# Two attention blocks on one core: V loaded through GpSimd's queue, loads in cycles of eight units, and one unit of eight transposed by the remainder's DMA

## The chip, the core and the metric

The kernel runs on one core of one Trainium2 chip. A core has TensorE (PE; its weight loads are listed as PEld), VectorE (DVE), ScalarE (ACT), GpSimd (POOL) and SyncE (SP), which run their own instruction streams and wait for each other on semaphores, and 16 DMA engines that move data between HBM and SBUF and within SBUF. The metric is the device time of one execution in microseconds. Before the change the median of three runs is 1215.2 us (1215.15 to 1217.5).

## What is computed

Two attention blocks A and B of the same shape, one after the other, with inputs of their own. The result is the concatenation of both along the last axis.

```
B, Sq, D = 16, 144, 448;  H, Sk, Dh = 16, 512, 256        # bf16
q      = (x @ wq).reshape(B, Sq, H, Dh).transpose(0, 2, 1, 3)
scores = einsum("bhqd,bhkd->bhqk", q, k_cache) * Dh ** -0.5
p      = softmax(scores, axis=-1)
o      = einsum("bhqk,bhkd->bhqd", p, v_cache)
out    = o.transpose(0, 2, 1, 3).reshape(B, Sq, H * Dh) @ wo
```

K and V are caches: 67 MB each for each block, read once.

## The kernel before

A *unit* is one pair of batch and head, 512 in all (256 for each block). Its 144 query rows are split in a main part of 112 rows (QA) and a *remainder* of 32 rows (QB). Four units' remainders fill 128 partitions, so the remainder is worked in groups G of four units, and two groups make a *cycle* SG of eight units (64 cycles).

What a unit goes through, with the lines of the kernel before:

- `t_q` (line 340): TensorE multiplies x by wq, eight matmuls into `qp_ps`; VectorE (353) or ScalarE (357) writes `qt_sb`.
- `t_sa` (476): the main part's scores, two matmuls into one of two `sa_ps` banks. `t_max` (488) on VectorE, `t_exp` (499) on ScalarE into `pa_sb`, `t_recip` (509) on VectorE, `t_norm` (517) on GpSimd, which multiplies P by the reciprocal of the row sum.
- `t_ta` (530): "TA", four transposes of P on TensorE into the `sa_ps` banks; `t_evac_pta` (540) copies them on VectorE into `pt_sb`.
- `t_pv` (563): P times V, eight matmuls into `ot_ps`; ScalarE (578, 580) writes them to `ring`.
- `t_op_piece` (601): the output projection, matmuls of `ring` with `wo_sb`, in pieces spread over the units; `t_evac_op` (619, 622) and `t_store` (630) write 36 blocks of rows.

For a cycle's remainder: `t_sb` (380) makes the scores of eight units in two `sb_ps` banks; `t_max_b` (393), `t_exp_b` (403), `t_recip_b` (413) and `t_norm_b` (421) make P in `pb_sb`. Its transpose goes one of two ways. In the cycles of the set `TB_SG`, `t_tb` (443, "TB") does it on TensorE and `t_evac_tb` (453) on VectorE copies it to `pbt_sb`. In the others `t_ptb_dma` (431) does it with a transposing DMA from SP, `pb_sb` to `pbt_sb`. In both ways `t_copy_ptb` (463) on GpSimd spreads it from `pbt_sb` into `pt_sb`, group by group.

Loads, all issued on SP's queue: `t_load_k` (307), a transposing DMA of 2 MB for a cycle; `t_load_v` (318), 1 MB for four units; `t_load_x` (297 and 298), two transposing DMAs for two batches (32 units); `t_load_wq` (276, 278) and `t_load_wo` (286).

The order is recorded by a loop over *slots* i (line 745 on). In slot i each engine's list gets the work of several units: the query projection of a unit about 8 further than the scores, the scores of unit i + lag, the norm of the unit whose scores were recorded one slot earlier, TA of unit i + 2 (`LT`), P V of unit i, and some pieces of the output projection. `LAGS` gives the lag by cycle: it begins at 7, drops to 5 and grows to 14. `sb_slot[SG]` is 8 SG - lag, the slot of the remainder's scores; `sa_slot[u]` that of a unit's scores. A small class (`_Sched`) derives the semaphore waits from what each instruction reads and writes, so a transfer into a buffer waits for the last reader of it. Each engine works through its list in order; SP too, so a load that waits holds up every load behind it.

When loads are recorded is planned in slots by `plan_x`, `plan_k`, `plan_v` and `plan_pb`. After the first eight cycles (`RAMP`) the plan runs in steps of two cycles (line 694): x, P, K, P, K and then four V in this order. There are two K buffers (`NK`), five V buffers (`NV`), fourteen for P (`NPA`), and one for `pbt_sb` (`NPBT`).

Of the kernel before, what the change touches and what calls it, by code (L numbers as in the profile page):

```python
# [122 lines left out]
def bass_concat_heads__mha_block_cached__gqa_block_cached__near_ridge_kernel(  # L123
# [24 lines left out]
    NU = Bn * H  # L148
# [14 lines left out]
    LAGS = (7, 5, 6, 7, 8, 9, 10, 11, 12, 13, 14)  # L163
    RAMP = 8
    TB_SG = set(range(RAMP)) | set(range(NSG // 2 - 4, NSG // 2 + 6))
    NK, NV, NXG = 2, 5, 2
    WO_AT = ((12, 18, 26, 33), (277, 277, 293, 293))
# [4 lines left out]
    NQT, NPA, NPB, NPT, NST, NSTB, NOST = 12, 14, 2, 8, 4, 2, 3  # L172
# [10 lines left out]
    with contextlib.ExitStack() as es:  # L183
# [14 lines left out]
        pb_sb = sb("pb_sb", [128, NPB, 2, SK], BF16)  # L198
        pt_sb = sb("pt_sb", [128, NPT, 4, SQ], BF16)
        pbt_sb = sb("pbt_sb", [128, NPBT, 2, 4, 128], BF16)  # L200
# [15 lines left out]
        for i in range(NV):  # L216
            sem_names.append("v%d" % i)
        for i in range(NXG):
            sem_names.append("xt%d" % i)
# [19 lines left out]
        def t_ident():  # L239
            ones = pa_sb[:, 0, 0:128]  # L240

            def e1(g):
                return g.memset(ones, 1.0)
            S.add(POOL, e1, writes=[(("pa", 0), "ones")], name="ones")

            def e2(g):
                return g.affine_select(ident[:], ones, pattern=[[1, 128]], compare_op=ALU.is_equal,
                                       fill=0.0, base=0, channel_multiplier=-1)
            S.add(POOL, e2, reads=[(("pa", 0), "ones")], writes=[("ident", 0)], name="ident")

# [61 lines left out]
        def t_load_v(G):  # L312
            pr, b, h0 = unit(4 * G)
            sl = G % NV
            src = vs[pr][b, h0:h0 + 4].rearrange("u (p c) d -> p u (c d)", p=128)

            def e(q):
                return q.dma_start(v_sb[:, sl, :, :], src).then_inc(sems["v%d" % sl], 16)
            S.add(SP, e, writes=[(("v", sl), G)], dma_sem="v%d" % sl, name="v%d" % G)
# [106 lines left out]
        def t_ptb_dma(SG):  # L426
# [3 lines left out]
            def e(q):  # L430
# [3 lines left out]
            S.add(SP, e, reads=[(("pb", psl, g), (2 * SG + g, 1)) for g in range(2)],  # L434
                  writes=[(("pbt", tsl, g), SG) for g in range(2)], dma_sem="pb%d" % tsl, name="pb%d" % SG)
# [56 lines left out]

        def t_exp(U):
            bank = U % 2
            sl = U % NST
            psl = U % NPA

            def e(a):
                return a.activation(pa_sb[0:QA, psl, :], sa_ps[bank][0:QA, :], AF.Exp,  # L499
                                    bias=stat[0:QA, NEG + sl:NEG + sl + 1], scale=1.0,  # L500
                                    accum_out=stat[0:QA, RSUM + sl:RSUM + sl + 1])
            S.add(ACT, e, reads=[(("sap", bank), ("s", U)), (("neg", sl), U)],
                  writes=[(("pa", psl), (U, 0)), (("rsum", sl), U)], banks=["sa%d" % bank], name="ex%d" % U)
# [8 lines left out]
        def t_norm(U):  # L512
            sl = U % NST
            psl = U % NPA

            def e(g):
                return g.tensor_tensor(pa_sb[0:QA, psl, :], pa_sb[0:QA, psl, :],  # L517
                                       stat[0:QA, RINV + sl:RINV + sl + 1].to_broadcast([QA, SK]), op=ALU.mult)
            S.add(POOL, e, reads=[(("pa", psl), (U, 0)), (("rinv", sl), U)], writes=[(("pa", psl), (U, 1))],
                  name="nm%d" % U)  # L520

        def t_ta(U):
            psl = U % NPA
# [114 lines left out]
        t_warm_zero()  # L638
        ta_bank = {}
        lag = [LAGS[min(n, len(LAGS) - 1)] for n in range(NSG)]  # L640
# [24 lines left out]
        def plan_k(at, SG):  # L665
            plan(at, sa_slot[8 * (SG - NK) + 7] + 1 if SG >= NK else s_min, sb_slot[SG], t_load_k, SG)
# [5 lines left out]
        def plan_pb(at, SG):  # L672
            if SG not in TB_SG:
                plan(at, sb_slot[SG] + 5, 8 * SG - 1, t_ptb_dma, SG)

        plan_x(s_min, 0)
        for hg in range(HG):
            plan(s_min + (0 if hg < 2 else 1), s_min, q_slot[4 * hg], t_load_wq, 0, hg)
            if hg == 1:
                plan_k(s_min, 0)  # L680
        plan_v(s_min + 2, 0)
        for n in range(1, RAMP + 2):
            at = max(sb_slot[n] - 6, sa_slot[8 * (n - NK) + 7] + 1) if n >= NK else s_min + 2
            if n == 3:
                plan_x(at, 1)
            if n == 6:
                plan_x(at, 2)
            plan_k(at, n)
            plan_v(at + 1, 2 * n - 1)
            plan_v(at + 1, 2 * n)  # L690
# [3 lines left out]
        for n in range(RAMP, NSG, 2):  # L694
            t = 8 * n
            XG = (t + 32) // (XB * H)
            if (t + 32) % (XB * H) == 0 and XG < NXGT:
                plan_x(t - 4, XG)
            plan_pb(t - 4, n)
            if n + 2 < NSG:  # L700
                plan_k(t - 3, n + 2)
            plan_pb(t + 2, n + 1)
            if n + 2 < NSG:
                plan_k(t + 2, n + 3)
            for j, at in enumerate((5, 5, 5, 8)):
                if 2 * n + 3 + j < NG:
                    plan_v(t + at, 2 * n + 3 + j)
        for hg in range(HG):
            lo = q_slot[NU - H + 4 * hg + 3] + 1
            plan((4.9, 4.9, 8, 11)[hg] + NU - 32, lo, q_slot[NU + 4 * hg], t_load_wq, 1, hg)  # L710
# [35 lines left out]
        while True:  # L746
# [16 lines left out]
            while stores and stores[0][1] <= i and (i % 16 in (9, 10, 11) or i >= NT - 4):  # L763
# [23 lines left out]
            if i % 8 == 1 and 0 <= i < NT:  # L787
                t_copy_ptb((i + 3) // 4)
            for u in sa_at.get(i - 1, ()):
# [3 lines left out]
            if 0 <= u < NT:  # L793
# [104 lines left out]
```

## Time and profile before

| | |
|---|---|
| median of three runs | 1215.2 us |
| the profiled execution | 1209.51 us |
| its span on the core | 1207.8 us |
| mean granted TensorE clock | 0.994 |
| DMA | 306.18 MB, 254 GB/s on the mean |

The rows of the costliest groups that the change touches:

| line, engine | operation | count | busy us | mean ns |
|---|---|---|---|---|
| 517 POOL | multiply P, main part | 512 | 531.4 | 1039 |
| 421 POOL | multiply P, remainder | 128 | 133.0 | 1039 |
| 463 POOL | copy `pbt_sb` to `pt_sb` | 128 | 78.0 | 610 |
| 530 PE | TA matmuls | 2048 | 185.9 | 212 |
| 443 PE | TB matmuls | 144 | 12.4 | 219 |
| 540 DVE | copy of TA | 512 | 191.0 | 373 |
| 453 DVE | copy of TB | 36 | 14.1 | 416 |
| 307 SP | K load, transposing DMA | 64 | | |
| 318 SP | V load | 128 | | |
| 431 SP | P of the remainder, transposing DMA | 46 | | |

The page gives for every engine the time in which it executes something, then the span in 40 slices, then the groups. TensorE's matmuls are pipelined, so the durations of a group overlap and add up to more than the time that they take on the chain. The chain of waits is followed back from the last instruction; it gives for each piece its start, its length and the engine and line. DMA issues are listed with the engine that issues them (SPq is SP's queue): the time of an issue is that of the queue's instruction, not that of the transfer; the time to landing is counted from the issue.

### The profile page before, as it was taken

The numbers are of one execution on the slowest core, as the hardware profiler recorded it, in microseconds if no ns is written. First come the engines' busy times: TensorE is split into PE (matmuls) and PEld (weight loads), VectorE is DVE, ScalarE is ACT, GpSimd is POOL, SyncE is SP. The second block draws the span as 40 slices with busy tenths as digits, with TensorE's granted clock in tenths as the row PEclk, the third lists the DMA queues.
The fourth block names the chain that finished last, engine by engine and source line by source line (L and its number), as shares of the span: only waits on it lengthen the run. The fifth ranks groups of instructions, "written<-read, shape, count | busy, mean of one in ns | idle before, by whom it ended". The sixth has DMA issues, their size and how long they took to land.

```text
span 1207.8 us, 33200 instructions
## 1 busy us (share of the span) xinstructions
PE 1167.9 (97%) x13612; PEld 875.3 (72%) x13612; DVE 743.6 (62%) x2088; ACT 747.8 (62%) x2213; POOL 727.0 (60%) x774
## 2 busy tenths in 40 slices
PE   6898999999999999999899999999999999999989
PEld 4676777777777777777577777777777777777766
DVE  3676666666666656666466665665666566566661
ACT  2565666666666666666466666666666666566662
POOL 1676576666666566666465665666666665666661
PEclk9999999999999999999899999999999999999999
DMA  9999999999999999999999899999999999999981
GB/s 243 284 262 294 283 277 188 253 264 269 268 283 206 264 253 293 259 263 245 288 249 255 249 265 277 261 279 251 268 236 248 253 292 274 231 251 252 249 207 56
DMA packets 679577, 306.18 MB, mean 254 GB/s; under 512 B 597504, under 2 KB 610304, under 8 KB 679424
## 3 DMA queue, kind: packets, MB, share of 16 engines
q1 hardware_dynamic: 679424, 304.05, 104.1%
q8 instruction: 107, 1.75, 0.6%
q14 instruction: 46, 0.38, 0.1%
HBM read 148.90 MB, written 4.13 MB: 127 GB/s over the span
## 4 chain that ended last, share of the span: by engine, by line
PE 81%; DMA 11%; POOL 3%; DVE 3%; SPq 1%; issue 1%; ACT 0%; DVEq 0%
PE ot_ps L563 18%; PE qp_ps L340 17%; PE sa_ps L476 17%; PE op_ps L601 16%; PE sa_ps L530 7%; DMA kt_sb<-in_B_k_cache_dram 6%; PE sb_ps L380 5%; DMA kt_sb<-in_A_k_cache_dram 5%; POOL pa_sb L517 2%; DVE stat L488 1%; SPq L307 1%; POOL pb_sb L421 1%; PE qp_ps L601 1%; PE sb_ps L443 0%; DVE qt_sb L353 0%
## 5 line engine op out<-in xcount | busy, mean ns | idle before, releaser
L517 POOL TENSOR_TENSOR pa_sb<-pa_sb,stat 112x512 bf16<-112x512 bf16 x512 | 531.4, 1039 | 453.0 <-DVE stat L509 427.4
L499 ACT ACTIVATE pa_sb<-sa_ps,stat 112x512 bf16<-112x512 f32 x512 | 352.1, 688 | 400.5 <-DVE stat L488 398.2
L488 DVE TENSOR_REDUCE stat<-sa_ps 112x1 f32<-112x512 f32 x512 | 353.8, 691 | 329.6 <-PE sa_ps L476 324.8
L340 PEld LDWEIGHTS qp_ps<-xt_sb,wq_sb 128*128 128x128 bf16 x4048 | 283.4, 98 | 81.6 <-DMA wq_sb<-in_A_wq_dram 3.6
L340 PE MATMUL qp_ps<-xt_sb,wq_sb 128*128 128x144 bf16 x4048 | 336.7, 226 | 5.0 <-DMA wq_sb<-in_A_wq_dram 4.7
L563 PE MATMUL ot_ps<-pt_sb,v_sb 128*128 128x144 bf16 x4096 | 341.5, 226 | 0.0
L476 PE MATMUL sa_ps<-kt_sb,qt_sb 128*112 128x512 bf16 x1024 | 312.6, 387 | 6.7 <-DVE pt_sb L540 5.2
L601 PE MATMUL op_ps<-wo_sb,ring 128*128 128x448 bf16 x1120 | 275.3, 353 | 0.0
L563 PEld LDWEIGHTS ot_ps<-pt_sb,v_sb 128*128 128x128 bf16 x4096 | 268.9, 98 | 0.4
L530 PEld LDWEIGHTS sa_ps<-ident,pa_sb 112*128 112x128 bf16 x2048 | 143.8, 97 | 119.0 <-ACT pa_sb L499 38.0
L540 DVE COPY pt_sb<-sa_ps 128x448 bf16<-128x448 bf16 x512 | 191.0, 373 | 19.8 <-PE sa_ps L530 19.8
L578 ACT ACTIVATE ring<-ot_ps 128x288 bf16<-128x288 f32 (+8 forms) x512 | 190.6, 372 | 19.2 <-PE ot_ps L563 19.2
L530 PE MATMUL sa_ps<-ident,pa_sb 112*128 112x112 bf16 x2048 | 185.9, 212 | 5.7 <-ACT pa_sb L499 5.7
L353 DVE TENSOR_SCALAR qt_sb<-qp_ps 128x288 bf16<-128x288 f32 x252 | 115.1, 457 | 93.4 <-PE qp_ps L340 91.6
L421 POOL TENSOR_TENSOR pb_sb<-pb_sb,stat 128x512 bf16<-128x512 bf16 x128 | 133.0, 1039 | 0.0
L476 PEld LDWEIGHTS sa_ps<-kt_sb,qt_sb 128*112 128x112 bf16 x1024 | 96.4, 130 | 46.3 <-issue 27.6
L357 ACT ACTIVATE qt_sb<-qp_ps 128x288 bf16<-128x288 f32 x254 | 105.3, 415 | 32.0 <-PE qp_ps L340 30.6
L601 PEld LDWEIGHTS op_ps<-wo_sb,ring 128*128 128x128 bf16 x1120 | 96.1, 98 | 31.9 <-issue 0.2
L499 ACT ACTIVATION_READ_ACCUMULATOR pa_sb<-sa_ps,stat 112x1 f32 x512 | 99.1, 193 | 0.0
L403 ACT ACTIVATE pb_sb<-sb_ps,stat 128x512 bf16<-128x512 f32 x128 | 88.5, 691 | 0.8
L393 DVE TENSOR_REDUCE stat<-sb_ps 128x1 f32<-128x512 f32 x128 | 87.2, 681 | 0.0
L463 POOL COPY pt_sb<-pbt_sb 128x512 bf16<-128x512 bf16 x128 | 78.0, 610 | 10.9 <-PE ot_ps L563 10.9
(33 smaller groups left out, 345.1 us busy)
## 6 DMA issues: line engine op xcount, KB each, us to landing
v_sb<-in_A_v_cache_dram SPq DMA_DIRECT2D x64, 1024.0 KB, 9.0
v_sb<-in_B_v_cache_dram SPq DMA_DIRECT2D x64, 1024.0 KB, 9.0
out_dram<-ost_sb SPq DMA_DIRECT2D x36, 112.0 KB, 9.5
wo_sb<-in_A_wo_dram SPq DMA_DIRECT2D x8, 448.0 KB, 9.3
wo_sb<-in_B_wo_dram SPq DMA_DIRECT2D x8, 448.0 KB, 5.3
wq_sb<-in_A_wq_dram SPq DMA_DIRECT2D x4, 768.0 KB, 6.0
wq_sb<-in_B_wq_dram SPq DMA_DIRECT2D x4, 768.0 KB, 10.5
pbt_sb<-pb_sb SPq DMA_TRANSPOSE x46, 4.7
```

Source lines behind the costliest of these rows:

```text
L340: ins = t.matmul(acc[:, dc * SQ:(dc + 1) * SQ], lhsT=wq_sb[:, kc, c0:c0 + 128], rhs=xt_sb[:, xsl, kc, xo:xo + SQ], start=(kc == 0 and dc = ...
L353: return v.tensor_scalar(qt_sb[:, sl, :, :], src, 1.0 / 16.0, None, op0=ALU.mult)
L421: return g.tensor_tensor(pb_sb[:, psl, G % 2, :], pb_sb[:, psl, G % 2, :], stat[:, RINVB + sl:RINVB + sl + 1].to_broadcast([128, SK]), op= ...
L476: ins = t.matmul(sa_ps[bank][0:QA, :].rearrange("q (k r) -> q k r", k=KR), lhsT=qt_sb[:, U % NQT, dc, 0:QA], rhs=kt_of(U, dc), start=(dc = ...
L488: return v.tensor_reduce(stat[0:QA, NEG + sl:NEG + sl + 1], sa_ps[bank][0:QA, :], axis=AX.X, op=ALU.max, negate=True)
L499: return a.activation(pa_sb[0:QA, psl, :], sa_ps[bank][0:QA, :], AF.Exp, bias=stat[0:QA, NEG + sl:NEG + sl + 1], scale=1.0, accum_out=stat ...
L517: return g.tensor_tensor(pa_sb[0:QA, psl, :], pa_sb[0:QA, psl, :], stat[0:QA, RINV + sl:RINV + sl + 1].to_broadcast([QA, SK]), op=ALU.mult)
L530: ins = t.transpose(pta_ps[bank][:, c * 128:c * 128 + QA], src[:, c, :], ident[0:QA, 0:QA])
L540: return v.tensor_copy(pt_sb[:, sl, :, 0:QA], pta_ps[bank][:, 0:512].rearrange("p (c q) -> p c q", c=4)[:, :, 0:QA])
L563: ins = t.matmul(ot_ps[ob][:, dc * SQ:(dc + 1) * SQ], lhsT=v_sb[:, vsl, j, c * DH + dc * 128:c * DH + (dc + 1) * 128], rhs=pt_sb[:, sl, c, ...
L578: ins = a.activation(ring[:, 2 * h:2 * h + 2, c0:c0 + n1], src[:, :, 0:n1], AF.Copy)
L601: ins = t.matmul(acc[0:m, 0:D], lhsT=ring[:, c, col0:col0 + m], rhs=wo_sb[:, c, :], start=(c == first), stop=(c == last))
```

## The change

- All V loads but the first are issued by GpSimd, in order with its arithmetic. K, x, P, the weights and the stores stay on SP.
- The plan runs in cycles of eight units: K of cycle SG is recorded as soon as its buffer can be free (one slot after the last scores of cycle SG - 2), P of the remainder five slots after the remainder's scores, V as soon as its buffer can be free plus one slot.
- The lag grows to 10 instead of 14 and begins at 5; the first phase is six cycles instead of eight. `TB_SG` is the first six cycles alone, so 6 cycles instead of 18 transpose the remainder on TensorE, and 58 instead of 46 use the DMA.
- `ADMA = (2,)`: in those 58 cycles the P of unit 2 of the eight is written to a third slice of `pb_sb` and goes through the same transposing DMA (three slices of 128 x 512 instead of two). `t_ta` and `t_evac_pta` of that unit are left out, and `t_copy_pta` on GpSimd copies the result from `pbt_sb` to `pt_sb`. Rows 112 to 127 of the slice are set to zero once at the start.
- Buffers: `NQT` 12 to 9, `NPA` 14 to 10, `NOST` 3 to 2; `pb_sb` and `pbt_sb` have a third slice. The times of the wq, wo and x loads and of the stores are set anew.

```
-    LAGS = (7, 5, 6, 7, 8, 9, 10, 11, 12, 13, 14)
-    RAMP = 8
-    TB_SG = set(range(RAMP)) | set(range(NSG // 2 - 4, NSG // 2 + 6))
+    LAGS = (5, 5, 6, 7, 8, 9, 10)
+    RAMP = 6
+    TB_SG = set(range(RAMP))
+    ADMA = (2,)
+    NPX = 2 + len(ADMA)
...
-    NQT, NPA, NPB, NPT, NST, NSTB, NOST = 12, 14, 2, 8, 4, 2, 3
+    NQT, NPA, NPB, NPT, NST, NSTB, NOST = 9, 10, 2, 8, 4, 2, 2
...
+        def t_pb_zero():
+            def e(v):
+                return v.memset(pb_sb[96:128, :, 2:NPX, :], 0.0)
...
-            S.add(SP, e, writes=[(("v", sl), G)], dma_sem="v%d" % sl, name="v%d" % G)
+                return q.dma_start(v_sb[:, sl, :, :], src).then_inc(sems["vs" if G == 0 else "v%d" % sl], 16)
+            S.add(SP if G == 0 else POOL, e, writes=[(("v", sl), G)], dma_sem="vs" if G == 0 else "v%d" % sl, name="v%d" % G)
...
-            S.add(SP, e, reads=[(("pb", psl, g), (2 * SG + g, 1)) for g in range(2)],
-                  writes=[(("pbt", tsl, g), SG) for g in range(2)], dma_sem="pb%d" % tsl, name="pb%d" % SG)
+            S.add(SP, e, reads=[(("pb", psl, g), (2 * SG + g, 1)) for g in range(2)] +
+                  [(("pb", psl, 2 + k), ("a", 8 * SG + j, 1)) for k, j in enumerate(ADMA)],
+                  writes=[(("pbt", tsl, g), SG) for g in range(NPX)], dma_sem="pb%d" % tsl, name="pb%d" % SG)
+
+        def by_dma(U):
+            return U % 8 in ADMA and U // 8 not in TB_SG
+
+        def t_copy_pta(U):
+            SG = U // 8
+            tsl = SG % NPBT
+            k = 2 + ADMA.index(U % 8)
+
+            def e(g):
+                return g.tensor_copy(pt_sb[:, U % NPT, :, 0:QA], pbt_sb[:, tsl, k, :, 0:QA])
+            S.add(POOL, e, reads=[(("pbt", tsl, k), SG)], writes=[(("pta", U % NPT), U)], name="cpta%d" % U)
...
+        def p_of(U):
+            if by_dma(U):
+                psl, k = (U // 8) % NPB, 2 + ADMA.index(U % 8)
+                return pb_sb[0:QA, psl, k, :], ("pb", psl, k), ("a", U)
+            psl = pa_slot[U]
+            return pa_sb[0:QA, psl, :], ("pa", psl), (U,)
...
+        def plan_pb(SG):
             if SG not in TB_SG:
-                plan(at, sb_slot[SG] + 5, 8 * SG - 1, t_ptb_dma, SG)
+                plan(sb_slot[SG] + 5, sb_slot[SG] + 5, 8 * SG - 2, t_ptb_dma, SG)
...
+        for XG in range(1, NXGT):
+            t = XB * H * XG
+            plan_x(t - (30 if XG < 2 else 33.5), XG)
+        for SG in range(NSG):
+            plan_pb(SG)
+            if SG >= NK:
+                plan_k(sa_slot[8 * (SG - NK) + 7] + 1, SG)
+        for G in range(NV, NG):
+            plan_v(4 * (G - NV) + 5, G)
...
-        for n in range(RAMP, NSG, 2):
-            t = 8 * n
-            XG = (t + 32) // (XB * H)
-            if (t + 32) % (XB * H) == 0 and XG < NXGT:
-                plan_x(t - 4, XG)
-            plan_pb(t - 4, n)
-            if n + 2 < NSG:
-                plan_k(t - 3, n + 2)
-            plan_pb(t + 2, n + 1)
-            if n + 2 < NSG:
-                plan_k(t + 2, n + 3)
-            for j, at in enumerate((5, 5, 5, 8)):
-                if 2 * n + 3 + j < NG:
-                    plan_v(t + at, 2 * n + 3 + j)
...
-            while stores and stores[0][1] <= i and (i % 16 in (9, 10, 11) or i >= NT - 4):
+            while stores and stores[0][1] <= i and (i % 8 in (7, 0, 1) or i >= NT - 4):
...
+            for k, j in enumerate(ADMA):
+                u = i + j - (1 if j > 2 else 0)
+                if (i - (1 if j > 2 else 0)) % 8 == 0 and 0 <= u < NT and by_dma(u):
+                    t_copy_pta(u)
...
-            if 0 <= u < NT:
+            if 0 <= u < NT and not by_dma(u):
                 ta_bank[u] = 1 - last_sa % 2 if sas else u % 2
                 t_ta(u)
                 t_evac_pta(u)
```

## The prediction

> **What bounds the kernel now.** I read the page first, then the chain of waits, then the waits of TensorE, then the loads on SP's queue. Busy shares and slices:
>
> ```profile
> PE 1167.9 (97%) x13612; PEld 875.3 (72%) x13612; DVE 743.6 (62%) x2088; ACT 747.8 (62%) x2213; POOL 727.0 (60%) x774
> ...
> PE   6898999999999999999899999999999999999989
> ```
>
> TensorE is idle for 1207.8 - 1167.9 = 39.9 us, nearly all at the start, at one place in the middle (slice 20) and at the end. In between a cycle of eight units is matmul behind matmul. A stretch of the chain (start, length, work):
>
> ```profile
> 562.86 0.50 PE qp_ps L340 x8
> 563.36 0.43 PE sa_ps L476 x2
> 563.99 0.50 PE ot_ps L563 x8
> 564.87 0.50 PE qp_ps L340 x8
> ...
> 574.42 0.45 PE sb_ps L443 x8
> ...
> 580.73 19.00 DMA kt_sb<-in_B_k_cache_dram
> ```
>
> Between the end of the scores (563.36 + 0.43 = 563.79) and the start of P V (563.99) stand 0.20 us: the four transposes of P on TensorE (TA, line 530). The eight transposes of the remainder (TB, line 443), where a cycle has them, take 0.45 us. At 580.73 the chain leaves TensorE: a K load took 19.00 us and TensorE stood still. Later on this chain the remainder's scores start at 766.86 and, eighteen cycles on, at 1090.53: a cycle is 323.67 / 18 = 18.0 us. Where the idle time lies (stretch, length, TensorE busy, then other engines, granted clock):
>
> ```profile
> 100.00:120.00 20.00, 16.15 (x181) 12.04 (x178) 11.11 (x32) 10.77 (x31) 10.48 (x12) 0.91 1.17 294
> ...
> 580.00:600.00 20.00, 14.09 (x173) 10.86 (x175) 10.15 (x30) 10.64 (x35) 10.29 (x11) 0.94 1.17 256
> 600.00:620.00 20.00, 20.00 (x216) 14.80 (x209) 11.87 (x34) 10.61 (x31) 11.01 (x12) 0.89 1.09 310
> ```
>
> A stall costs twice: the idle 5.9 us at 580 and then a clock of 0.94 and 0.89, worth 0.06 x 20 + 0.11 x 20 = 3.4 us. What the remainder's scores waited for (idle us, times), and what SP's queue does (min/median/max ns of an issue):
>
> ```profile
>   DMA kt_sb<-in_B_k_cache_dram: 10.5, 7
>   DMA kt_sb<-in_A_k_cache_dram: 5.2, 3
> ...
> L307 SPq DMA_TRANSPOSE kt_sb<-in_B_k_cache_dram x32: 7577/8647/16566, 580.7 to 1143.2; - x32
> ...
> L318 SPq DMA_DIRECT2D v_sb<-in_B_v_cache_dram x64: 367/507/1897, 605.8 to 1178.6; - x64
> ...
> L431 SPq DMA_TRANSPOSE pbt_sb<-pb_sb x46: 1232/1364/5315, 182.8 to 1177.3; - x46
> ```
>
> So 15.7 us were lost waiting for K. A K load lands in 9.6/12.0/19.0 us (min, median, max), a V load in 9.0, the remainder's transposing DMA in 3.1/4.7/11.3. K issues stretch to 16.6 us when V is ahead of them in the same queue.
>
> **The change, part by part.** Sums are against the profiled run, 1209.5 us, 1.7 more than its span; the runs' median is 1215.2, so I add 5.7 at the end.
>
> 1. *TA taken from TensorE.* In the 58 cycles that use the transposing DMA (6 of 64 do not), one unit of eight has no TA: 58 x 0.20 = -11.6. The bounds are 0.20 (the gap) and 0.36 (its four matmuls run alone): -11.6 to -20.9; TensorE is back to back, so I take the gap. VectorE also loses 58 copies of 0.37, off the path.
>
> 2. *TB cycles cut from 18 to 6.* 12 x 0.45 = -5.4. VectorE's 24 copies out of PSUM (0.39 us each) go too, off the path.
>
> 3. *V on GpSimd's queue.* 127 issues leave SP and stand among GpSimd's multiplications. GpSimd per cycle of eight: 10 multiplications x 1.039 + 2 copies x 0.609 + the new copy of unit 2 (448 of 512 columns, 0.53) = 12.14 us; a cycle after part 1 is 18.0 - 0.2 = 17.8, so 5.66 are left for two V issues: 2.83 each. No row shows a DMA issued by GpSimd. Below stands the same load on SP, 0.37; above SP's longest issues of one load, K's 7.6. The run structure (512 runs of 2 KB) is that of SP's V rows, so I stay near 0.5 and take 1.0, since GpSimd needs 1.04 us for the elementwise work on a block that VectorE reduces in 0.69. The 127 us are covered by GpSimd's idle time, 453 us before line 517 alone; without that cover each 0.1 us above 2.83 costs 0.2 x 58 = 11.6. The issue waits for P V two slots earlier, and behind it stand norms that TensorE wants seven slots (15 us) later, and the copies of the remainder, wanted one slot later. Cost 0.
>
> The Trainium skill (SBUF — State Buffer, SBUF: two separate sides) says that a DMA issued from GpSimd starves for descriptors while VectorE runs an operation that takes both SBUF ports. The trace of before has no lock to show: line 517 takes 1037/1039/1042 ns although VectorE's copies run beside it. By that rule V issues would stretch by VectorE's copies, 0.37 us each; it feeds the first rival.
>
> 4. *K with SP nearly to itself.* SP now issues per cycle one K (7.6), one P (1.36 x 1.5 = 2.0), some 0.6 of stores and 0.6 of x: 10.8 of 17.8 us. K goes out when the last score of the cycle but one before it frees its buffer and is wanted eight slots later, some 18 us, against 12.0 to land and 19.0 at worst. The engines keep the same bytes plus 58 x 3 - 46 x 2 = 82 slices of 131 KB; at K's 2.1 MB in 7.6 us that is 0.47 us each, 39 us of engine time. Fine stretches at 784 to 822 show engines idle for about 5 of 36 us (0 GB/s at 784 and 819 to 821). So K should mostly be in time. Of 15.7 us stalled and 3.4 + 1.8 of clock after it (100 to 120: 0.09 x 20), 20.9 in all, I take -12, because the first cycles are short (15.6 us at 56.17 and 71.80) and their DMA stays full. Bounds 0 and -20.9.
>
> The Trainium skill (DMA: Bandwidth & Descriptors, Issuing engines are not separate DMA queues) holds that issuing from several engines saves only sequencer time, since all share 16 engines. By it part 4 gives little, and the forecast would be 12 us higher. Against it here stands the row of K issues of 16.6 us, which is SP held up behind V.
>
> 5. *P of three slices.* It waits for two remainder norms and unit 2's norm on GpSimd, lands 4.7 + 0.6 us later, and is wanted by GpSimd's copy four slots (8.9 us) after. Behind that copy in GpSimd's order wait norms and V, and P V of units 0 to 3 waits for the copy. In cycles with an x load (14 of the 58) SP has K, two x transposes (4.4 + 1.3 median), then P: 7.6 + 5.7 + 2.0 = 15.3 of 17.8, so P is late now and then. Bounds: 0, and 14 x (11.3 + 0.6 - 8.9 = 3.0) = 42; I take 14 x 0.3 = +4, since the median fits.
>
> 6. *Scores 10 units ahead instead of 14, first lead 5 instead of 7, smaller buffers.* The same matmuls; the tail has four units fewer in store, and its idle time is 3.1 us of 1150 to 1180 now. Bounds -3 and +6, I take +2. The added memset of pb_sb lies under the 3.4 us that TensorE waits at the start: 0.
>
> Sum: 1209.5 - 11.6 - 5.4 - 12 + 4 + 2 = 1186.5, plus 5.7 = 1192. Its own range: 1176 (all K stalls gone, nothing added) to 1208 (K stalls kept).
>
> **Rivals.**
>
> *A. GpSimd becomes the bound.* If a V issue takes t, its cycle is 12.14 + 2t. At 3.1 us the cycle is 18.3, 0.3 above today's, and 58 x 0.3 = 17 has eaten the gains of parts 2 and 4 (that of part 1 is gone with TensorE's lead); at 3.5 it is 19.14, +1.14 x 58 = +66, less 17: 1209.5 + 49 + 5.7 = 1264; at 4.05, half way between 0.5 and 7.6, 1328. For it: no row prices it. Against it: SP's 0.5 for the same load is six times below the point.
>
> *B. The transposes come late, slower than before.* V and K now mix on the engines instead of following one another; P, which stood before K in SP's order, has K's tail and V beside it. Place: GpSimd's copy of pbt_sb. If P lands at 9.9 us instead of 5.3, each cycle is 1.0 us late: +58, less 29 from parts 1, 2 and 4 = +29: 1244. It decides from a landing of 8.9 + 29/58 = 9.4. For it: landings of 11.3 exist, and V's landing of 9.0 shows long queues. Against it: the median 4.7 and idle engine time.
>
> *C. The load order changes nothing.* K waits as now, and P in x cycles takes 1.2 us each: 1209.5 - 17 + 14 x 1.2 = 1209.3, 1215 as a median. For it: the engines are as full as before; against: K issues of 16.6 us behind V.
>
> **How the numbers follow.** Forecast 0.62, A 0.12, B 0.19, C 0.07. A measurement here tells 0.2% (2.4 us) from no change. Faster: the forecast and a little of C, 0.63; same: most of C, 0.06; slower: A and B, 0.31. Range: from 1176 up to 1245, which takes in C and the milder half of B and leaves out A, half of B and the edges of the forecast, about 0.2.
>
> **What would show it.** Right: cycles of about 17.8 us in the middle; 1816 transposes on line 558's group and 48 on the TB group; waits of the remainder's scores for K under 6 us; GpSimd busy with gaps; V issues under 2.83 us. Wrong: GpSimd's multiplications without idle time (A); P V waiting for GpSimd's copy or that copy for the P transfer (B); K waits as large as 15 us (C).

## The result, and the profile after

The changed kernel takes 1337.5 us at the median (1321.6 to 1343.9), the kernel before beside it 1216.3: a ratio of 1.095 with a 95% interval of 1.086 to 1.105. Ratios, here and below, leave out a run more than 1.5% above the fastest of its kernel (here that of 1343.9), so they can differ a little from the ratio of the medians. It is slower by about 120 us where 23 us less were forecast, and outside the range of 1176 to 1245. The profiled execution took 1339.0 us with a span of 1337.3, so it stands for the median; the mean granted clock fell from 0.994 to 0.948.

Busy time, the slices of TensorE and of the granted clock, the DMA total and the two load queues, from the page after:

```profile
PE 1187.4 (89%) x13284; PEld 879.1 (66%) x13284; DVE 719.4 (54%) x2007; ACT 744.4 (56%) x2213; POOL 848.7 (63%) x959
...
PE   6375889999999899969888877999999799999989
...
PEclk9697989999999899989888898999999899999999
...
DMA packets 689430, 316.88 MB, mean 237 GB/s; under 512 B 639872, under 2 KB 652672, under 8 KB 689280
...
q1 hardware_dynamic: 654736, 181.62, 78.5%
q0 software_dynamic: 34544, 133.18, 33.3%
```

TensorE has 328 matmuls fewer (13612 before) and yet 19.5 us more of busy time. It is idle for 1337.3 - 1187.4 = 149.9 us instead of 39.9. Idle time and busy time together, 110.0 + 19.5, are the 129.5 us by which the span grew. q0 is GpSimd's queue with V; q1 is SP's. The DMA engines moved 10.7 MB more at 237 GB/s instead of 254. (The rate is the bytes divided by the span, so it falls with any loss of time.)

The waits of the matmuls (what waited for what, us in total, times, longest):

```profile
PE sb_ps L388 <- DMA kt_sb<-in_A_k_cache_dram: 68.9, 11, 20.6
POOL pt_sb L484 <- DMA pbt_sb<-pb_sb: 63.3, 14, 8.2
...
PE ot_ps L591 <- issue: 33.8, 7, 6.7
...
PE sb_ps L388 <- DMA kt_sb<-in_B_k_cache_dram: 22.2, 7, 4.5
```

The remainder's scores (line 388 now) wait 91.1 us for K, against 13.9 before. (The prediction's 15.7 was read from a list that adds the idle time of the weight loads to that of the matmuls; the matmuls alone stood still for 13.9.) P V (line 591) waits 33.8 us with no releaser in the records ("issue"), and the row of GpSimd (POOL) says where that begins: GpSimd's copy of `pbt_sb` waits for the remainder's transposing DMA. Each of the ten longest waits of P V ends 0.1 us after such a copy, which itself had waited 2.6 to 8.2 us.

The loss has its places. The table gives the time from the start of the remainder's scores of one cycle to those of another, in the profiled executions; the two kernels in the middle are the changed one with V issued by SP and by ScalarE (next section).

| cycles | before | V on SP | V on ScalarE | changed |
|---|---|---|---|---|
| 0 to 8 | 143.0 | 148.3 | 173.5 | 192.1 |
| 8 to 24 | 286.2 | 301.4 | 298.5 | 304.0 |
| 24 to 40 | 298.9 | 318.2 | 342.1 | 346.4 |
| 40 to 60 | 359.4 | 378.4 | 371.9 | 373.6 |

GpSimd's queue costs 44 us more than SP's in the first eight cycles and 28 in cycles 24 to 40, and in the others 3 and -5 us, next to nothing. In the two costly stretches the weights of a block are loaded beside K and V; that this sets the loss in is not shown. Of the 91.1 us of waits for K, 47.7 lie in the first 200 us: the waits from 0 to 100 and from 100 to 200 us, and two windows of 4 us in the longest of them (stretch, length, busy time of PE, PEld, DVE, ACT and POOL, clock, DMA share, GB/s):

```profile
PE sb_ps L388 <- DMA kt_sb<-in_A_k_cache_dram: 22.2, 2, 20.6
...
PE sb_ps L388 <- DMA kt_sb<-in_A_k_cache_dram: 25.5, 3, 17.8
```

```profile
44.00:48.00 4.00, 0.00 (x0) 0.00 (x0) 0.00 (x0) 0.00 (x0) 0.00 (x0) 0.50 1.12 65
48.00:52.00 4.00, 0.00 (x0) 0.00 (x0) 0.00 (x0) 0.00 (x0) 0.00 (x0) 0.50 1.36 79
```

No engine computes there, and the DMA engines, at shares of 1.12 and 1.36, move 65 and 79 GB/s. On the chain of waits a smaller place in block B looks so (start, length, work):

```profile
702.62 0.50 PE ot_ps L591 x8
703.13 0.50 PE qp_ps L348 x8
703.63 0.58 PE sa_ps L497 x2
704.24 23.35 DMA kt_sb<-in_B_k_cache_dram
727.63 1.90 PE sb_ps L388 x16
...
737.31 2.95 issue
740.26 1.12 PE ot_ps L591 x8
```

The K load issued at 704.24 took 23.35 us, where 18 were to be had. The sixteen matmuls behind it take 1.90 us instead of 0.98 at 755.02 on the same chain, and the next P V 1.12 instead of 0.50: the clock is about halved after a stall (0.50 in every window of 1 us from 726 to 732). SP's queue and one row of GpSimd in the same stretch (start, length, issue; in brackets the wait before it):

```profile
704.24 14.56 SPq L315 DMA_TRANSPOSE kt_sb<-in_B_k_cache_dram  x1
718.84 1.29 SPq L305 DMA_TRANSPOSE xt_sb<-in_B_x_dram  x1
720.18 1.38 SPq L306 DMA_TRANSPOSE xt_sb<-in_B_x_dram  x1
721.61 0.58 SPq L658 DMA_DIRECT2D out_dram<-ost_sb  x1
722.24 12.90 SPq L439 DMA_TRANSPOSE pbt_sb<-pb_sb  x1
735.19 9.41 SPq L315 DMA_TRANSPOSE kt_sb<-in_B_k_cache_dram  x1
```

```profile
739.55 0.61 POOL L484 COPY pt_sb<-pbt_sb 128x512 bf16<-128x512 bf16 x1 [7.08 <-DMA pbt_sb<-pb_sb]
```

Behind the late K the transfer of P, whose issue takes 1.3 us at least, takes 12.90; GpSimd waits 7.08 us for it and P V comes at 740.26. The granted clock in this stretch (columns as above):

```profile
700.00:720.00 20.00, 19.85 (x237) 14.88 (x235) 13.13 (x37) 12.67 (x36) 15.30 (x17) 1.00 1.16 221
720.00:740.00 20.00, 11.30 (x107) 7.34 (x104) 6.27 (x18) 6.66 (x19) 4.29 (x5) 0.80 1.16 166
```

On the mean the DMA engines are as busy as in the stretch before (1.16; the share passes 1 where the times of an engine's packets overlap) and move 166 GB/s instead of 221. The mean hides idle time. From 728 to 738 us, in slices of 0.25 us (busy tenths):

```profile
DMA  0100027861114396998999998968999000000067
```

The engines are nearly idle at 728 to 729.25, at 730.25 to 731 and at 735.75 to 737.5 us, while the transfer of P is under way (issued at 722.24, landed 17.3 us later). So not all of the delay is a lack of room on the engines; what else holds P there is not shown. V's issues are cheap (min/median/max ns of an issue; in block A the first takes 927 and no other above 801):

```profile
L326 POOL DMA_DIRECT2D v_sb<-in_B_v_cache_dram x64: 789/789/801, 677.8 to 1290.5; - x64
```

### The profile page after: what moved, and what is told of

Same layout as the page of the kernel before. It is cut to its first block, busy times and chain, and to the rows that moved or that the text cites. A ratio compares the mean times of both kernels' runs of the same rounds, so it can differ in the third digit from the quotient of the medians.

```text
span 1337.3 us, 32498 instructions
## 1 busy us (share of the span) xinstructions
PE 1187.4 (89%) x13284; PEld 879.1 (66%) x13284; DVE 719.4 (54%) x2007; ACT 744.4 (56%) x2213; POOL 848.7 (63%) x959
## 2 busy tenths in 40 slices
DMA packets 689430, 316.88 MB, mean 237 GB/s; under 512 B 639872, under 2 KB 652672, under 8 KB 689280
## 4 chain that ended last, share of the span: by engine, by line
PE 61%; DMA 31%; issue 2%; DVE 2%; SPq 1%; ACT 1%; POOL 1%; DVEq 0%
DMA kt_sb<-in_A_k_cache_dram 20%; PE ot_ps L591 14%; PE sa_ps L497 13%; PE op_ps L629 13%; PE qp_ps L348 13%; DMA kt_sb<-in_B_k_cache_dram 11%; PE sa_ps L558 5%; PE sb_ps L388 4%; DVE stat L509 1%; SPq L315 1%; ACT pb_sb L528 1%; POOL pa_sb L546 1%; PE qp_ps L629 0%; SPq L284 0%; ACT pa_sb L528 0%
## 5 line engine op out<-in xcount | busy, mean ns | idle before, releaser
L546 POOL TENSOR_TENSOR pa_sb<-pa_sb,stat 112x512 bf16<-112x512 bf16 x454 | 470.2, 1037 | 407.7 <-DVE stat L538 381.1
L528 ACT ACTIVATE pa_sb<-sa_ps,stat 112x512 bf16<-112x512 f32 x454 | 312.2, 688 | 472.5 <-DVE stat L509 470.4
L591 PE MATMUL ot_ps<-pt_sb,v_sb 128*128 128x144 bf16 x4096 | 351.3, 230 | 37.5 <-issue 33.8
L497 PE MATMUL sa_ps<-kt_sb,qt_sb 128*112 128x512 bf16 x1024 | 320.9, 396 | 4.6 <-DVE pt_sb L568 3.0
L591 PEld LDWEIGHTS ot_ps<-pt_sb,v_sb 128*128 128x128 bf16 x4096 | 279.5, 100 | 52.3 <-issue 38.8
L558 PEld LDWEIGHTS sa_ps<-ident,pa_sb 112*128 112x128 bf16 x1816 | 131.3, 99 | 109.5 <-ACT pa_sb L528 19.5
L568 DVE COPY pt_sb<-sa_ps 128x448 bf16<-128x448 bf16 x454 | 169.0, 372 | 10.4 <-PE sa_ps L558 10.4
L558 PE MATMUL sa_ps<-ident,pa_sb 112*128 112x112 bf16 x1816 | 168.6, 216 | 2.8 <-ACT pa_sb L528 1.3
L388 PE MATMUL sb_ps<-kt_sb,qt_sb 128*32 128x512 bf16 x1024 | 73.7, 412 | 91.2 <-DMA kt_sb<-in_A_k_cache_dram 68.9
L388 PEld LDWEIGHTS sb_ps<-kt_sb,qt_sb 128*32 128x32 bf16 x1024 | 22.6, 99 | 116.2 <-DMA kt_sb<-in_A_k_cache_dram 43.4
```

The costliest lines, as they stand in the source:

```text
L388: ins = t.matmul(sb_ps[jj // 4][32 * j:32 * j + 32, :].rearrange("q (k r) -> q k r", k=KR), lhsT=qt_sb[:, U % NQT, dc, QA:SQ], rhs=kt_of(U ...
L497: ins = t.matmul(sa_ps[bank][0:QA, :].rearrange("q (k r) -> q k r", k=KR), lhsT=qt_sb[:, U % NQT, dc, 0:QA], rhs=kt_of(U, dc), start=(dc = ...
L528: return a.activation(dst, src, AF.Exp, bias=stat[0:QA, NEG + sl:NEG + sl + 1], scale=1.0, accum_out=stat[0:QA, RSUM + sl:RSUM + sl + 1])
L546: return g.tensor_tensor(dst, dst, stat[0:QA, RINV + sl:RINV + sl + 1].to_broadcast([QA, SK]), op=ALU.mult)
L558: ins = t.transpose(pta_ps[bank][:, c * 128:c * 128 + QA], src[:, c, :], ident[0:QA, 0:QA])
L568: return v.tensor_copy(pt_sb[:, sl, :, 0:QA], pta_ps[bank][:, 0:512].rearrange("p (c q) -> p c q", c=4)[:, :, 0:QA])
```

## The experiments

Ratios are against the kernel before on the same chip; "+x us" is (ratio - 1) x 1215.2. Waits are those of TensorE's matmuls or, where said, of GpSimd.

### Which part costs it

**V back on SP's queue**, all else as in the changed kernel:

```
-            S.add(SP if G == 0 else POOL, e, writes=[(("v", sl), G)], dma_sem="vs" if G == 0 else "v%d" % sl, name="v%d" % G)
+            S.add(SP, e, writes=[(("v", sl), G)], dma_sem="v%d" % sl, name="v%d" % G)
```

> The changed kernel with every V load back on SP's queue, at the same places of the plan; nothing else. Queue theory (V on a second queue runs beside K on the same engines and takes their time, so K and P land late): K lands in about 12 us again, waits of the remainder's scores for K fall from 154 us to under 30, and the time comes to 1190 to 1225. Plan theory (loads in cycles of eight and a lead of 10 leave K too little time, whatever the queue): the time stays above 1300. Slice theory (the third slice of the transposing DMA holds up SP and GpSimd): above 1280, with GpSimd still waiting about 60 us for P.

Measured 1267.3 us, 1.0442 (1.0399 to 1.0485): +54. More than half of the loss is gone with the queue alone, and K waits fall from 91.1 to 20.1 us. (The 154 us of the expectation add the idle time of the weight loads.) None of the three ranges held: K lands at 15.9 us at the median, not 12, and what is left is not small. GpSimd waits 108.6 us for P, in 43 of the 58 cycles that use its DMA.

**The kernel before with V on GpSimd's queue**, its plan unchanged:

```
-            S.add(SP, e, writes=[(("v", sl), G)], dma_sem="v%d" % sl, name="v%d" % G)
+            S.add(SP if G == 0 else POOL, e, writes=[(("v", sl), G)], dma_sem="vs" if G == 0 else "v%d" % sl, name="v%d" % G)
```

> The kernel before with V (all but the first load) on GpSimd's queue, at the same places of its plan; nothing else. Queue theory: K's landing goes from 12 to 16 us or more and the time from 1215 to 1260 or more. Plan theory and slice theory: 1205 to 1225, since neither the plan nor the slice is in it.

Measured 1226.3 us, 1.0091 (1.0064 to 1.0118): +11, 1.3 us above the range of the plan and slice theories and far below that of the queue theory. The queue that costs 116 - 54 = 62 us more than SP's in the new plan costs 11 in the old one, so it is not the queue by itself: the plan that it meets has a part in it.

**The changed kernel without the third slice:**

```
-    ADMA = (2,)
+    ADMA = ()
...
-        t_pb_zero()
```

> The changed kernel without the third slice: unit 2 of every cycle is transposed on TensorE again, the transposing DMA has two slices. Queue theory: between 1300 and 1345, K still lands in about 17 us. Slice theory: 1190 to 1230, and GpSimd's 63 us of waiting for P go.

Measured 1317.7 us (1313.1 to 1360.6), 1.0836 (1.0801 to 1.0871): +101. That is in the queue theory's range. The slice costs some 15 to 20 us here and saves nothing, though the two intervals touch (1.086 to 1.105 with it). The profiled execution of this kernel was the 1360.6 one, 43 us above its median, so no row of it is used.

**The new plan alone**, V on SP and no third slice (both edits above):

> The changed kernel with V on SP and without the third slice: the new plan, lags and fewer TB cycles alone. Plan theory (on SP each V now stands ahead of the next K and of P, where before four V stood behind them): 1250 or more, and GpSimd still waits for P about 100 us. If instead the slice made the 52 us that the run with V on SP lost, this one comes to 1200 to 1225.

Measured 1229.4 us, 1.0124 (1.0075 to 1.0172): +15, between the two ranges. TensorE's matmuls wait 15.8 us for K and 19.9 for GpSimd's copy of P.

**The third slice alone, in the old plan**, V on SP. For the room it takes `NQT`, `NPA` and `NOST` go down by one (12, 14, 3 to 11, 13, 2); `TB_SG`, the lags and the plan are those of before:

```
+    ADMA = (2,)
+    NPX = 2 + len(ADMA)
```

> The kernel before with its own plan and lags and V on SP, and the third slice alone added for its 46 cycles (buffers NPA 13, NQT 11, NOST 2 to make room). If the slice itself is bad (it holds up SP and GpSimd), 1225 or more. If it does what the prediction's part 1 says, 46 x 0.2 = 9 us go: 1203 to 1210.

Measured 1225.5 us, 1.0076 (1.0044 to 1.0108): +9, in the first theory's range. The 46 cycles with the slice need 184 transposes less on TensorE, whose busy time falls from 1167.9 to 1164.1, but K waits grow from 13.9 to 30.8 us.

**V issued by ScalarE** (`ACT` instead of `POOL` in the changed kernel):

> The changed kernel with V issued by ScalarE instead of GpSimd, still a second queue. If a second queue as such does the harm (V's packets go ahead of K's), K lands in 16 us or more and the time stays near 1300. If it is the queue of GpSimd (in the loads-alone run K beside V from GpSimd took 144.9 us, from ScalarE 108.0), the time falls to 1220 to 1270, by K landings near 14 us.

Measured 1299.1 us, 1.071 (1.0647 to 1.0773): +86, between SP's +54 and GpSimd's +116. K lands at 17.4 us at the median, as the first theory had it. Against SP's queue ScalarE's costs 32 us, and GpSimd's another 30; why GpSimd's costs more is not shown.

### What the queues do to each other

**Loads alone.** Nothing is computed; six stages, each of eight K loads of 2.1 MB, sixteen V loads of 1.05 MB, or both, with the kernel's buffers:

```
        stage(1, True, None)
        stage(2, False, "sp")
        stage(3, False, "pool")
        stage(4, True, "sp")
        stage(5, True, "pool")
        stage(6, True, "act")
```

> Loads alone, no attention is computed and the output is not the reference's: six stages one after the other, of 8 K loads (2 MB, transposing) and 16 V loads (1 MB): K alone on SP; V alone on SP; V alone on GpSimd; K and V by turns on SP; K on SP beside V on GpSimd; K on SP beside V on ScalarE's queue. If the engines only share their time, the stages with both take as long as the sum of K alone and V alone (about 8 x 7.6 + 16 x 2.7 = 104 us), from whatever queues. If the mix itself costs (queue theory in its stronger form), the fifth stage is 20% or more longer than the sum, and the fourth is not. If it is GpSimd's descriptors and not the second queue, the sixth is like the fourth.

| stage | from - to, us | length |
|---|---|---|
| K alone | 0.7 - 67.5 | 66.8 (8.35 for a K) |
| V alone, SP | 67.5 - 114.1 | 46.6 (2.9 for a V) |
| V alone, GpSimd | 114.1 - 161.1 | 47.0 |
| K and two V by turns on SP | 161.1 - 275.8 | 114.7 |
| K on SP, V on GpSimd | 275.8 - 420.7 | 144.9 |
| K on SP, V on ScalarE | 420.7 - 528.7 | 108.0 |

By turns on one queue the loads take the sum of both alone (113.4). Beside V from GpSimd they take 28% longer than that, beside V from ScalarE 5% less. First the DMA rows of K alone (0 to 67 us), then of a stretch with V on GpSimd (297 to 319 us): packets and rate, and for a queue its packets, MB and the time of its packets as a share of 16 engines:

```profile
DMA packets 65791, 16.78 MB, mean 250 GB/s; under 512 B 65791, under 2 KB 65791, under 8 KB 65791
...
q1 hardware_dynamic: 65791, 16.78, 115.7%
```

```profile
DMA packets 2548, 2.03 MB, mean 92 GB/s; under 512 B 2189, under 2 KB 2189, under 8 KB 2548
...
q1 hardware_dynamic: 2167, 0.55, 113.5%
q0 software_dynamic: 381, 1.47, 16.7%
```

K comes in packets of 256 B (16.78 MB / 65791), V from GpSimd in packets of 3.9 KB. A K packet alone holds an engine for 1.157 x 16 x 67 us / 65791 = 18.9 ns; in the second stretch for 1.135 x 16 x 22 us / 2167 = 184 ns. The engines are as busy as before and move a third as much. Beside ScalarE's queue such a stretch did not come in this run: 384 GB/s at 425 to 465 us, with 6816 packets of V and 7136 of K, about as many of the one as of the other, as if the queues took turns packet by packet; K, with the small packets, got 1.83 MB in 40 us, 46 GB/s. (In another such stretch, below, the packets are 4334 to 6872.)

**V held back until K has landed** (V on GpSimd, its issue made to wait for the K load of its cycle):

```
+        def v_reads(G):
+            j = G // 2
+            return [(("kt", j % NK), j)] if G >= NV else []
...
-            S.add(SP if G == 0 else POOL, e, writes=[(("v", sl), G)], dma_sem="vs" if G == 0 else "v%d" % sl, name="v%d" % G)
+            S.add(SP if G == 0 else POOL, e, reads=v_reads(G), writes=[(("v", sl), G)], dma_sem="vs" if G == 0 else "v%d" % sl, name="v%d" % G)
...
-            plan_v(4 * (G - NV) + 5, G)
+            plan_v(8 * (G // 2) - 13 + G % 2, G)
```

> The changed kernel with V on GpSimd's queue, but each pair of V loads is recorded later and waits until the K load that is under way has landed, so that the two do not run together (after the first five V). Theory of the mix: K lands in 11 to 13 us again and the time falls to 1200 to 1250. If the new plan is at fault and not the overlap, it stays above 1290.

Measured 1502.5 us at the median of 1489.4 to 1530.0, a ratio of 1.226 (1.220 to 1.232): above the 1290 of the second theory, but for a reason that neither had, since neither reckoned with where the wait stands. It is in GpSimd's list, with norms and copies behind it. GpSimd's waits in the profiled execution (1514.2 us, 24 above the two shortest):

```profile
POOL v_sb L330 <- DMA kt_sb<-in_B_k_cache_dram: 166.4, 26, 14.4
...
POOL v_sb L330 <- DMA kt_sb<-in_A_k_cache_dram: 136.5, 23, 15.0
```

That is 303 us of GpSimd in which no norm was made. The edit did not keep V and K apart either: V is issued at 808.66 and 810.46 us and the next K at 810.43, and K lands at 18.9 us at the median. So the run says nothing of the queues; it shows what a DMA wait on a computing engine costs.

**The loads again, with V paced** by one, two or five buffers:

```
-        stage(1, True, None)
...
+        stage(1, True, "pool", 1)
+        stage(2, True, "act", 1)
+        stage(3, True, "pool", 2)
+        stage(4, True, "act", 2)
+        stage(5, True, "pool", 5)
```

> Loads alone, no attention is computed and the output is not the reference's: five stages of 8 K on SP beside 16 V, the V from GpSimd with one under way at a time, from ScalarE with one, from GpSimd with two, from ScalarE with two, from GpSimd with five. If stretches of 95 GB/s come with GpSimd's queue whatever the depth, the first, third and fifth stage take 125 us or more and the second and fourth 108 to 115. If they come from many V under way, only the fifth does.

The five stages took about 137, 122, 132, 158 and 112 us. Neither pattern of the expectation came. With one buffer the V loads run one by one up to the end of their stage, so its length is partly V's own. The run refutes the reading that the slow stretches belong to GpSimd's queue: the longest one here, 414 to 432 us, came with ScalarE's, and the last stage, the same loads that took 144.9 us above, took 112. The DMA rows of these two stretches, 414 to 432 and 550 to 600 us:

```profile
DMA packets 4289, 1.98 MB, mean 110 GB/s; under 512 B 3791, under 2 KB 3791, under 8 KB 4289
...
q1 hardware_dynamic: 3777, 0.96, 100.4%
q10 hardware_dynamic: 512, 1.02, 25.2%
```

```profile
DMA packets 11206, 18.47 MB, mean 369 GB/s; under 512 B 7126, under 2 KB 7126, under 8 KB 11206
...
q0 software_dynamic: 4334, 16.71, 87.4%
q1 hardware_dynamic: 6872, 1.76, 19.4%
```

In the second, V runs at 334 GB/s, nearly its rate alone (1.05 MB in 2.9 us is 360), and K at 35. So two things happen when K runs beside V of another queue: K is pushed back while V lasts, which costs no bandwidth, and at times the engines fall to about 100 GB/s, which does. What sets the second in stays open.

### Is there room in the DMA engines at all

**New plan, V on SP but recorded behind P** (V no longer ahead of P in SP's order), without and with the third slice:

```
-            plan_v(4 * (G - NV) + 5, G)
+            plan_v(8 * (G // 2) - 13 + G % 2, G)
```

> The new plan alone (V on SP, no third slice) with the two V loads of a cycle recorded right behind P on SP's queue instead of one ahead of K and one ahead of P. If the order on the queue made the plan's loss (1229), K lands in 11 to 13 us, GpSimd's waits for P fall from 52 us to under 10, and the time comes to 1195 to 1212. If the shorter lead (10) or the single K per cycle made it, it stays at 1222 or more.

> The same with the third slice. If the slice lost 38 us (1267 against 1229) only because P stood behind a V and K behind P, it now gains what TensorE is spared, 58 x 0.2 = 12 us against the run without it: 1185 to 1205. If the slice's longer transfer is the cost itself, it is 10 us or more above the run without it.

Without the slice 1223.9 us, 1.0083 (1.0054 to 1.0111): +10, in the second theory's range, and not clear of the +15 with the other order. GpSimd's wait for P falls from 52.1 to 11.9 us, and the wait of the scores for K rises from 15.8 to 28.1. With the slice 1236.9, 1.0176 (1.0148 to 1.0204): +21. This is the cleanest trial of the third slice: P lands in 4.4 us at the median and 8.5 at most, TensorE is busy for 1159.2 us, 8.7 less than in the kernel before, and the kernel is slower, by 13 us than without the slice, as the second theory of the expectation had it. In cycles 40 to 60 a cycle takes 18.3 us with the slice, 17.9 without and 18.0 in the kernel before. Its chain by engine, and SP's queue in the middle:

```profile
PE 49%; DMA 45%; DVE 2%; SPq 1%; ACT 1%; issue 1%; POOL 0%; DVEq 0%
```

```profile
813.93 13.89 SPq L315 DMA_TRANSPOSE kt_sb<-in_B_k_cache_dram  x1
827.87 0.58 SPq L658 DMA_DIRECT2D out_dram<-ost_sb  x1
828.49 1.43 SPq L439 DMA_TRANSPOSE pbt_sb<-pb_sb  x1
829.97 1.49 SPq L326 DMA_DIRECT2D v_sb<-in_B_v_cache_dram  x2
831.50 13.19 SPq L315 DMA_TRANSPOSE kt_sb<-in_B_k_cache_dram  x1
844.73 1.52 SPq L439 DMA_TRANSPOSE pbt_sb<-pb_sb  x1
```

One issue ends where the next begins: SP's round from K to K is 17.6 us, about as long as the 17.8 us that TensorE was to need for a cycle. DMA has 45% of the chain, 11% in the kernel before.

**Three K buffers** (new plan, V on SP, no slice; one V buffer and one for P less and a lag of 9 for the room; four wq loads of block B one slot later):

```
-    LAGS = (5, 5, 6, 7, 8, 9, 10)
+    LAGS = (5, 5, 6, 7, 8, 9)
...
-    NK, NV, NXG = 2, 5, 2
+    NK, NV, NXG = 3, 4, 2
...
-    NQT, NPA, NPB, NPT, NST, NSTB, NOST = 9, 10, 2, 8, 4, 2, 2
+    NQT, NPA, NPB, NPT, NST, NSTB, NOST = 9, 9, 2, 8, 4, 2, 2
...
+        plan_k(sb_slot[0] + 4, 2)
...
-            plan_v(4 * (G - NV) + 5, G)
+            plan_v(8 * (G // 2) - 12 + 4 * (G % 2), G)
```

> The new plan with V on SP and no third slice, but three K buffers instead of two (four V buffers and a lead of 9 to make room; V recorded when its buffer comes free). If K is late because it may start only when the cycle but one before has freed its buffer (the wait as such), the waits of the remainder's scores for K go to under 5 us after the first 200 us and the time comes to 1185 to 1207. If the DMA engines are simply full (K, two V, P and the rest take nearly a cycle of TensorE), more buffers hardly help: 1212 to 1230.

Measured 1224.5 us, 1.0085 (1.0057 to 1.0113). Waits of TensorE and GpSimd:

```profile
POOL pt_sb L484 <- DMA pbt_sb<-pb_sb: 99.9, 40, 11.2
...
PE ot_ps L591 <- POOL pt_sb L484: 29.1, 8, 7.7
```

The scores wait for K only 1.0 us now, and the time is what it was with 28 us of such waits: they have become waits for P (29.1 us) and V (4.5). That is the second theory's range, and speaks against K's short lead as the cause. The reading that fits is that the engines spend on K earlier what P and V then miss; that the queue's order delays P is not excluded.

**TB alone** (the kernel before with `TB_SG` cut to its first eight cycles):

```
-    TB_SG = set(range(RAMP)) | set(range(NSG // 2 - 4, NSG // 2 + 6))
+    TB_SG = set(range(RAMP))
```

> The kernel before with the remainder of cycles 28 to 37 transposed by DMA too (TB_SG is the first eight cycles alone), nothing else. By the prediction's part 2 TensorE is spared 10 x 0.45 = 4.5 us: 1208 to 1212. If the DMA is as short as TensorE there, where the weights of the second block are loaded, the K waits around 580 us grow: 1214 to 1225.

Measured 1217.5 us over ten runs, 1.0023 (1.0007 to 1.0039): +2.8. That is the second theory's range, by another wait: those for K hardly grow (15.4 us), but P V waits 8.2 us for P in the middle, where the block changes and the weights are loaded. TensorE was spared eighty transposes.

## Why the prediction was wrong

The runs can be put in one table: the bytes that the DMA engines moved in the profiled execution, their mean rate, and the time.

| kernel | MB | GB/s | ratio | wait for K, us | waits of P V other than for V, us | clock |
|---|---|---|---|---|---|---|
| before | 306.18 | 254 | 1 | 13.9 | 0 | 0.994 |
| TB alone | 308.79 | 254 | 1.002 | 15.4 | 8.2 | 0.990 |
| slice alone | 312.17 | 255 | 1.008 | 30.8 | 0 | 0.992 |
| plan alone | 309.31 | 253 | 1.012 | 15.8 | 19.9 | 0.986 |
| plan, V behind P | 309.31 | 254 | 1.008 | 28.1 | 1.8 | 0.984 |
| plan, three K buffers | 309.31 | 253 | 1.008 | 1.0 | 30.7 | 0.989 |
| plan, V behind P, slice | 316.88 | 256 | 1.018 | 50.9 | 4.6 | 0.989 |
| plan, slice | 316.88 | 251 | 1.044 | 20.1 | 50.0 | 0.978 |
| before, V on GpSimd | 306.18 | 250 | 1.009 | 16.4 | 0.8 | 0.990 |
| changed, V on ScalarE | 316.88 | 244 | 1.071 | 53.2 | 49.5 | 0.962 |
| changed | 316.88 | 237 | 1.095 | 91.1 | 37.3 | 0.948 |

With V on SP's queue the rate is 251 to 256 GB/s whatever else is done. Being bytes by span, it shows no bound by itself; the idle time of the engines does. In windows of 4 us between 20 us and the last 20, the kernel before has its DMA engines under half busy in 68 us, the slice alone in 56, and the new plan on SP's queue, in its five versions, in 8 to 24. So the kernel before was bound by TensorE, and DMA had some 6% of the span to spare. The time grows with the bytes, but less than they do: at 254 GB/s the 10.7 MB are 42 us and cost 21 in the best order. The bytes are not all, either: the plan alone moves 1% more than the kernel before and leaves 16 us of the 68; what fills the engines there is not shown. An estimate of the engines' time for a cycle: K and two V 14.3 (by turns, nothing else under way), P 1.4 and x 0.7 (by their issues), and weights and stores 0.8 (4 wq loads of 768 KB and 8 wo of 448 KB for each block, 36 stores of 112 KB, at V's rate, over 64 cycles), 17.2 us of the 18.0 that a cycle takes. The third slice adds 0.5 us (0.131 MB at K's 0.25 MB/us) while TensorE's cycle falls to 17.8: 17.7 of 17.8.

The runs also split the 116 us: 21 with V on SP behind P, another 33 with V ahead of P on the same queue, and another 62 with V on GpSimd's queue.

*Parts 1 and 2, TA and TB taken from TensorE, -11.6 and -5.4.* The sizes were right as work: TensorE's busy time falls by 8.7 us with V behind P, at a clock 0.5% lower, which by an estimate (0.005 x 1159) hides about 6 more, 15 in all of the 17. They were wrong as time. Each brought nothing alone (+9 and +2.8): the same edits hand the DMA engines 6.0 and 2.6 MB there, 10.7 in the changed kernel, and the waits for K and P grew by 17 and 8 us.

*Part 3, V on GpSimd, cost 0.* The price was near: 0.79 us for an issue where 1.0 was taken and 2.83 was the bound, so GpSimd is not the bound (63% busy) and rival A falls. (The 7.6 us that stood as its upper bound, as SP's longest issue, is the shortest of K's in the row 7577/8647/16566.) No issue is longer than 801 ns in block B beside VectorE's copies. What the Trainium skill says under "SBUF — State Buffer, SBUF: two separate sides", of descriptors that starve, did not show in these issues; but it is no test, since the example there is a copy from SBUF to SBUF and the copies of 0.37 us here read PSUM (`sa_ps`). The prediction applied the rule to copies to which it may not apply. What was priced nowhere is the effect on the other queue: +54 with V on SP, +86 on ScalarE, +116 on GpSimd.

*Part 4, K with SP nearly to itself, -12.* This is the step that failed. It forecast that 12 of 20.9 us of K stalls and clock go. The stalls grew from 13.9 to 91.1 us: to 20.1 with the plan and the slice on SP's queue, and by 71 more with V on GpSimd's. The sum held no cost for K and V that share the engines from two queues. It took K's shortest issue, 7.6 us, for its transfer, where a K alone takes 8.35 and K and its cycle's two V 14.3, and read idle engines off one favourable stretch (5 of 36 us, 14%, where the whole kernel has 68 of 1160, 6%). It named the short first cycles, with their full DMA, as a limit of the gain; they are where the largest loss stands, 44 us of the queue's. It had the 39 us for the 82 slices in hand and left them out of the sum as covered. K lands at 12.9/17.9/39.4 us instead of 9.6/12.0/19.0, about its 18 us. SP's queue being free was no help: K's issue, meant to be shorter without V ahead, has a median of 12.3 to 12.7 us instead of 8.6 to 9.9. The rule cited there, from the Trainium skill (DMA: Bandwidth & Descriptors, Issuing engines are not separate DMA queues), was nearer than the row of 16.6 us that was set against it: a second issuing engine brought nothing. The runs go further, since it lost 32 to 62 us in this plan. That row was also misread: the issue of 16.6 us is the one at 580.73, and in front of it on SP's queue stand the weight loads of block B, the last V having gone out 9 us earlier.

*Part 5, P of three slices, +4.* Its upper bound was +42. P lands in 3.6/6.6/19.1 us, the copy of unit 2 took 0.56 us as reckoned (0.53), and P V waits 37.3 us. The step used landings of the old order, where P stood ahead of K; with V on SP the new order alone, without the slice, has P at 7.0 at the median. The slice itself costs 13 us in the best order, where the prediction had -11.6 and +4 for it.

*Part 6, the lag of 10 and the buffers, +2.* Not separated from the plan, which as a whole, with part 2 in it, costs +15, or +10 with V behind P. The lag alone was not tried: the old plan's slots are laid out for 14.

*The clock* was in the sum for the stalls that were to go, not for new ones. TensorE's 19.5 us more of busy time, with some 17 us of work taken away, make about 36 us by an estimate. The loss is then 110 us of new idle time and 36 of clock behind it, less the 17 spared.

*The range.* With the K stalls kept and part 6 at its +2 the sum is 1204, not 1208; nothing hangs on it.

*Rival B* was right in kind, transposes that come late, and in its sign; it had the price of P alone, +29, and no mechanism that lowers the rate of all loads. Rival C's line, that the engines are as full as before, was the one to follow: it got 0.07.

What stays open: what sets in the stretches of 92 to 110 GB/s. They came with GpSimd's queue and with ScalarE's, and stayed away in a repetition. Between the changed kernel and the same with V on SP, windows of 4 us under 130 GB/s with the engines over 90% busy add up to 52 us against 8, and with ScalarE's queue to 40; the kernel before has 24 us of them without harm, and with its V on GpSimd's queue 8. In the changed kernel 20 of the 52 us lie in the first 92. A cause within the engines is not shown, nor why the loss stands in the stretches where weights are loaded. No version that was run beat the kernel before.

## What to carry to other kernels

Where one engine is 97% busy, add up the DMA engines' time as well: by the estimate above it was 17.2 of the 18.0 us of a cycle here, and no version that moved work from TensorE to DMA paid. Price a transfer by its time on the DMA engines, measured alone and in its mix, not by its issue; and count idle DMA time over the whole kernel, not in one stretch. A second queue brought no time here when one queue kept the engines full (108 to 145 us for loads that take 115 by turns, +32 and +62 us in the kernel), and it takes away the order between loads: large packets overtook the small ones of a transposing load on which the next step waits. Look for the loss by stretches: most of this queue's stood in 24 of the 64 cycles.

## What the hardware showed unexpectedly

- A V load of 1.05 MB costs GpSimd 0.79 us of issue in every one of block B's 64 (789 to 801 ns), 0.75 us in most of the runs of loads alone; its packets are 3.9 KB.
- A transposing K load runs at 250 GB/s alone, at 35 to 46 beside V of another queue, V meanwhile at 334 to 338.
- Engines over 90% busy can move 92 to 110 GB/s, with a K packet of 256 B holding an engine for 184 ns instead of 18.9, and the same loads can take 144.9 us or 112.
- After a stall of 4.5 us, TensorE's granted clock is 0.50 for some us (726 to 732 in the changed kernel): the same sixteen matmuls take 1.90 us instead of 0.98.
